# Weight pairs of the last three products: load into two kinds of rooms, with urgent works and a mended joint in the plan

## The chip, the cores and the metric

The kernel runs on one core of a Trainium2 chip. The metric is the device time of one execution in microseconds, the median of the runs; lower is better.

## The reference

Three parts follow each other, all in fp32.

```python
attn = softmax(mask(q @ k.T / 8)) @ v          # 4 x 8 heads x 576 x 64; heads 0-3 see 32 keys back, 4-7 every fourth of 128
x = attn as [2304, 512]
h = x @ w_in                                    # first feed-forward, 512 -> 1024
solu = h * softmax(h); ln = layernorm(solu) * g_ln
x = ln @ w_out                                  # 1024 -> 512
h = x @ w_in2                                   # second feed-forward, 512 -> 2048
g = h * sigmoid(1.702 * h)
out = g @ w_out2                                # 2048 -> 512
```

The change lies in the second feed-forward.

## The kernel before

Products are made of fp32 values split in a high and a low part (hi, lo), so that each product of two blocks is three matmuls for each 128 rows of the sum: hi by hi, hi by lo, lo by hi.

**Tiling.** The 2304 tokens of the second feed-forward are three sets p = 0, 1, 2 of two blocks of 384 tokens. Each set goes through an h stage and then an o stage.

- h stage: eight quads q. A quad multiplies a 2x2 arrangement of blocks by Strassen's scheme with seven products m = 0 to 6 (`h_prod`, L659) of six matmuls, 128x384 each, in four accumulators: two in one two-bank tile hX (tag A of PSUM, tile hx) and two in hZW (tag B, tile hz). Between products the sums are formed by p1 (ACT, L664), u2 (L667), u3 (L671), c22 (L676), c21 (L679) and c12 (L682) on VectorE: m=4 goes into the bank that p1 reads, m=5 needs u3, m=6 needs c22. Then come the sigmoids (`h_sig`, ACT, L688) and the multiplications (`h_mul`, VectorE, L693, L695 and L697 for its parts 0, 1 and 2) that make g. Part 0 is the last to read hX. The inputs of the products are yc (hi by ACT, lo by VectorE, L645) and the weights ws (`quad_load`, L607), four loads a quad.
- o stage of p=0: plain products (`o_plain`, L741), 12 matmuls each, for eight steps jj, two halves and two token blocks b. Block 0 adds up in oa (tag A, both banks of one tile), block 1 in ob (tag B, four tiles). In the same stage the weights of the o stage are read as raw tiles from the input, split in hi and lo (hl tiles) and stored for later.
- o stage of p=1 and p=2: seven products again (`o_prod`, L772), six matmuls for each of the eight jj. The first four, m=0 to 3, run jointly over the eight jj with whole weights wo (`o_load`, L721). The last three, m=4, 5, 6, follow one after the other, each over all eight jj, with weights w that are loaded for a pair of jj at a time (`o_load2`, L758, tiles w2_p_m_jj, two DMAs of 256 KB for a pair): four pairs a product, 144 matmuls in all.
- The operands of the o stage, gs, are the hi part by ACT (L711) and the lo part by VectorE (L714), in five buffers. Sums of g (L707) stand ahead of some of them.

**Order.** A list scheduler (class `Plan`) sets the order of all works. A work has a rank, an engine or several, a cost, the works it comes after, slots it takes and slots it gives back, and a lag until others can use its result. At each time every free engine gets the work of lowest rank that can start. The works are then written out by their planned start, and each engine runs its own in that order. So a work that is not ready holds up all behind it on its engine, whatever the plan had thought.

**Rooms.** Weights lie in rooms of 128x1024. Nine have the slot name hl (`hl_tile`): ws, wo and split weights use them. Three have the name raw: raw weights use them, and in p=1 and p=2 the pairs w. The slots A (2) and B (4) are the banks of PSUM. SyncE issues all DMAs, in order; a load whose room is not free holds up the stores and loads behind it.

In the plain o stage of before the slots A and B are taken by the product of jj = 0 and half 0, and in the o stage of p=1 and p=2 by the product of jj = 0. Another product of the same accumulator was free to stand ahead of it in the plan; `first` in `o_plain` and `o_prod` follows the order that comes out.

Of the kernel before, what the change touches and what calls it, by code (L numbers as in the profile page):

```python
# [9 lines left out]
F32R = mybir.dt.float32r  # L10
# [8 lines left out]
P = 128  # L19
# [30 lines left out]
class Work:  # L50

    def __init__(self, n, rank, can, after, take, give, lag):
        self.key, self.can, self.lag = (rank, n), can, lag
        self.after, self.take, self.give = [w for w in after if w is not None], take, give
        self.start = self.done = None


class Plan:  # L60
# [11 lines left out]
    def order(self):  # L72
# [6 lines left out]
        while any(left.values()):  # L79
# [4 lines left out]
            for eng, works in left.items():  # L84
                while free[eng] <= t:
                    for w in works:
                        if all(a.done is not None and a.done <= t for a in w.after) and \
                                all(slots[s] >= w.take.count(s) for s in w.take) and \
                                (slots["port"] or not w.can[eng][2]) and \
                                all(t + w.can[eng][0] <= max(free[e], t) + c for e, (c, _, _) in w.can.items()):  # L90
                            break
                    else:
                        break
# [33 lines left out]
def attention_moe_kernel(ctx, tc, qk, qk_last, v, v_last, masks, w_in, w_out, g_ln, w2_in, w2_out, out):  # L127
# [623 lines left out]

    def o_load2(p, m, jj):

        t = stage[0].tile([P, 2, 2, 2 * P], F32R, tag="raw", bufs=NRAW, name=f"w2_{p}_{m}_{jj}")
        at_ = (2, 4, 14)[m - 4] * P
        for k in range(2):
            w2t[m, jj + k] = t[:, k]
            nc.sync.dma_start(f32(t[:, k]), wd["o", jj + k].rearrange("p (d c) -> p d c", d=2)[:, :, at_:at_ + 2 * P])  # L758
# [261 lines left out]
    for p in range(3):  # L1020
# [4 lines left out]
        for n, q in enumerate(QUADS):  # L1025
# [18 lines left out]
            for m in range(7):  # L1044
# [26 lines left out]
                for key in held if m == 6 else ():  # L1071
                    hl_end[key] = w
            muls[q] = [s0, s1, s2]
        last_m = [prods[QUADS[-1], m] for m in range(7)]
        y_free = last_m
# [11 lines left out]
        for jj in range(NQ if p == 0 else 0):  # L1087
# [14 lines left out]
            for b in range(2):  # L1102
                for half in range(2):
# [4 lines left out]
                            give=("gs", "hl", "hl") if b and half else ("gs",))  # L1108
                    now[jj, 2 * half + b] = x
            for d in range(2):  # L1110
                hl_end[(("o", jj, d), 0) if ("o", jj, d) in KEEP else (p, "o", jj, d)] = x
                if ("o", jj, d) in KEEP:
                    x.after.append(stored[("o", jj, d), 0])
# [13 lines left out]
        for jj in range(NQ):  # L1127
# [15 lines left out]
            for m in range(4):  # L1143
                x = add(r, "PE", 1.042, lambda p=p, jj=jj, m=m: o_prod(p, jj, m), loads + [ops[m], prods[QUADS[-1], 3]],
                        take=(("A",), ("A",), ("B", "B"), ("B", "B"))[m] if jj == 0 else (),
                        give=("gs", "hl", "hl") if m == 3 else ("gs",))
                now[jj, m] = x
            for d in range(2):
                hl_end[p, "o", jj, d] = x
        end_ = [[now[jj, m] for jj in range(NQ)] for m in range(4)]  # L1150

        def store(c, ws):
            add(r, "SP", 1.3, lambda p=p, c=c: o_store(p, c), ws, give=("sg",), lag=2.0)
# [5 lines left out]
        for d in range(2):  # L1159
            c22.append(add(r, "DVE", 0.53, lambda p=p, d=d: o_out(p, 0, d), end_[3] + [u3[d]] + c22, give=("u3",),  # L1160
                           take=() if d else ("sg",)))
        store(0, c22)
        wait = {4: p1, 5: u3, 6: c22}
        for m in (4, 5, 6):
            xs_ = []
            for jj in range(NQ):
                r = r0 + 10 * (NQ * (m - 3) + jj)
                if jj % 2 == 0:
                    w = add(r - 60, "SP", 1.7, lambda p=p, m=m, jj=jj: o_load2(p, m, jj),
                            [stored[("o", jj + k, d), part] for k in range(2) for d in range(2) for part in range(2)] +  # L1170
                            [now[1, 0]], take=("raw",), lag=2.0)
                if m == 4:
# [5 lines left out]
                else:  # L1178
                    op = operand(jj, m, 1, 1, muls[jj] + [gsum[jj, 0], gsum[jj, 2], gsum[jj, 3]], give=("g",))
                x = add(r, "PE", 1.042, lambda p=p, m=m, jj=jj: o_prod(p, jj, m), [w, op] + wait[m] + end_[3],  # L1180
                        give=("gs", "raw") if jj % 2 else ("gs",))
                xs_.append(x)
# [190 lines left out]
```

## Time and profile before

| | us |
|---|---|
| runs | 684.74 (median), 684.17, 687.91 |
| profiled execution | 682.37 |
| its span | 680.6 |
| TensorE busy in the span | 653.5 (96%) |
| VectorE busy | 522.7 (77%) |
| ACT busy | 387.7 (57%) |

The durations come from the profiled execution, whose span leaves out 1.8 us around it. The second feed-forward begins at about 300 us: p=0 until 438.55, p=1 until 558.05, p=2 to the end. In a timeline a row that says x12 is a run of 12 instructions of one kind that lie close together, and the time in brackets is how long the engine had waited ahead of it and for whom.

### The profile page before, as it was taken

To read this page: it belongs to the slowest core of one execution; us is meant where nothing else is said; L and a number is where in the kernel's file an instruction comes from. 1 tells how busy PE (TensorE), PEld (TensorE's weight loads), DVE (VectorE), ACT (ScalarE), POOL (GpSimd) and SP (SyncE) were. 2 spreads that over 40 slices of the span, in tenths; PEclk is the share of its full clock that TensorE was granted. 3 is DMA by queue.
4 is the path that set the end of the run, shared out by engine and by line. 5 is a ranking of instruction groups with operands and counts; after the bars stand their busy time and mean duration, and the time that the engine had idled before them with its cause. 6 is when DMAs were issued, how large, how long until landed. Compare 5 with 4: busy or idle time off the path is not lost.

```text
span 680.6 us, 12937 instructions
## 1 busy us (share of the span) xinstructions
PE 653.5 (96%) x4921; PEld 616.4 (91%) x4921; DVE 522.7 (77%) x948; ACT 387.7 (57%) x789; POOL 127.6 (19%) x148
## 2 busy tenths in 40 slices
PE   6788999999999999999997999999999999999997
PEld 5666898888888899999997999999999989999996
DVE  3999968775676899789666899387699848668783
ACT  4898877675566786865335676243366424334552
POOL 0305464362433452523000000000000000000000
PEclk9999999999999999999998999999999999999999
DMA  9998226544322667985674877876799865678655
GB/s 292 309 306 259 73 85 213 187 140 149 100 65 89 245 210 266 325 313 196 248 271 160 332 270 249 323 268 227 276 311 317 281 199 213 222 264 321 194 180 192
DMA packets 58254, 155.55 MB, mean 229 GB/s; under 512 B 6608, under 2 KB 21968, under 8 KB 58192
## 3 DMA queue, kind: packets, MB, share of 16 engines
q1 hardware_dynamic: 58192, 154.72, 66.6%
q8 instruction: 39, 0.64, 0.4%
q14 instruction: 23, 0.19, 0.1%
HBM read 118.53 MB, written 36.18 MB: 227 GB/s over the span
## 4 chain that ended last, share of the span: by engine, by line
PE 86%; DMA 6%; DVE 4%; ACT 2%; issue 1%; SPq 0%; POOL 0%; POOLq 0%; ACTq 0%; DVEq 0%
PE h L465 15%; PE hz L659 15%; PE y L538 13%; PE hx L659 11%; PE oz L772 8%; PE ox L772 7%; PE ob L741 5%; PE oa L741 5%; DMA w<-wdo 3%; PE lt L516 2%; PE ptp L309 2%; PE xt L325 2%; PE s L228 1%; DMA y<-in_qk_dram 1%; DMA raw_('o', 1, 1)_3957<-in_w_out_dram 1%
## 5 line engine op out<-in xcount | busy, mean ns | idle before, releaser
L711 ACT CAST gs<-g 128x384 fp32r<-128x384 f32 x144 | 73.2, 513 | 71.8 <-PE oz L772 26.1
L659 PE MATMUL hz<-yc,ws 128*128 128x384 f32 x576 | 109.1, 337 | 0.0
L659 PEld LDWEIGHTS hz<-yc,ws 128*128 128x128 f32 x576 | 102.0, 190 | 0.2 <-DVE g L676 0.2
L714 DVE TENSOR_TENSOR gs<-g,gs 128x384 fp32r<-128x384 f32 x144 | 78.4, 555 | 19.4 <-ACT gs L711 18.8
L659 PE MATMUL hx<-yc,ws 128*128 128x384 f32 x432 | 83.4, 335 | 0.9 <-DVE yc L645 0.5
L538 PE MATMUL y<-lnh,wo_h 128*128 128x256 f32 x288 | 83.0, 288 | 0.0
L538 PE MATMUL y<-lnh,wo_l 128*128 128x256 f32 x288 | 81.5, 283 | 0.0
L538 PE MATMUL y<-lnl,wo_h 128*128 128x256 f32 x288 | 81.5, 283 | 0.0
L659 PEld LDWEIGHTS hx<-yc,ws 128*128 128x128 f32 x432 | 75.4, 188 | 1.8 <-DVE yc L645 0.8
L465 PE MATMUL h<-wi_h,xh 128*128 128x512 f32 x144 | 59.0, 410 | 0.0
L465 PE MATMUL h<-wi_l,xh 128*128 128x512 f32 x144 | 56.4, 392 | 0.0
L465 PE MATMUL h<-wi_h,xl 128*128 128x512 f32 x144 | 56.4, 392 | 0.0
L538 PEld LDWEIGHTS y<-lnh,wo_h 128*128 128x128 f32 x288 | 55.1, 191 | 1.0
L538 PEld LDWEIGHTS y<-lnl,wo_h 128*128 128x128 f32 x288 | 55.2, 192 | 0.3
L538 PEld LDWEIGHTS y<-lnh,wo_l 128*128 128x128 f32 x288 | 55.1, 191 | 0.0
L688 ACT ACTIVATE sg<-g 128x768 f32<-128x768 f32 (+1 forms) x48 | 32.9, 686 | 31.8 <-DVE g L679 27.5
L688 ACT ACTIVATE sg<-hx 128x384 f32<-128x384 f32 x24 | 11.8, 492 | 49.7 <-PE hx L659 46.8
L772 PE MATMUL oz<-gs,w 128*128 128x384 f32 x192 | 34.9, 337 | 2.0 <-DMA w<-wdo 1.3
L772 PE MATMUL oz<-gs,wo 128*128 128x384 f32 x192 | 36.7, 335 | 0.0
L772 PE MATMUL ox<-gs,wo 128*128 128x384 f32 x192 | 36.5, 334 | 0.0
L772 PEld LDWEIGHTS oz<-gs,w 128*128 128x128 f32 x192 | 33.1, 188 | 3.4 <-issue 2.5
L301 POOL TENSOR_TENSOR t<-t,sx 128x768 f32<-128x768 f32 (+1 forms) x17 | 23.7, 1392 | 65.0 <-DVE sx L296 25.1
(391 smaller groups left out, 1408.9 us busy)
## 6 DMA issues: line engine op xcount, KB each, us to landing
ws<-wdq SPq DMA_DIRECT2D x48, 512.0 KB, 4.8
wo<-wdo SPq DMA_DIRECT2D x37, 512.0 KB, 5.5
ws<-wdq SPq DMA_DIRECT2D x48, 384.0 KB, 5.2
w<-wdo SPq DMA_DIRECT2D x48, 256.0 KB, 4.4
qk<-in_qk_dram SPq DMA_DIRECT2D x14, 528.0 KB, 5.5
v<-in_v_dram SPq DMA_DIRECT2D x14, 384.0 KB, 4.1
y<-in_w_in_dram SPq DMA_DIRECT2D x9, 512.0 KB, 5.0
wdq<-y SPq DMA_DIRECT2D x9, 512.0 KB, 3.2
```

The lines of the kernel that those rows point to most:

```text
L301: eng.tensor_tensor(t, t, wide(sms.pop(n), t.shape[1]), ALU.mult)
L309: nc.tensor.transpose(ps[:, j * P:j * P + P], t[:, 4 * h + j, :], ident)
L325: nc.tensor.matmul(ps[64 * h:64 * h + 64, w * QW:w * QW + QW], vW[4 * b + u][:, h, w, :], pt[:, h, w * QW:w * QW + QW], start=True, stop=True)
L465: nc.tensor.matmul(hps[i][:, half, :], x[:, kt, :], w[:, kt, fs], start=(kt == 0 and j == 0), stop=(kt == KT - 1 and j == 2))
L516: nc.tensor.transpose(ps[:, j, :], es[i][:, f * P:f * P + P], ident)
L538: nc.tensor.matmul(yps[g, dm][:, 0:n], w[:, f, ds_], x[:, f, 0:n], start=(f == 0 and j == 0), stop=(f == NF1 - 1 and j == 2))
L659: nc.tensor.matmul(ps[:, 0:TB2], quad_weights(q, m, kk, a), yc2[m][:, x, kk, :], start=(m < 4 and kk == 0 and i == 0), stop=(kk == 1 and i ...
L688: nc.scalar.activation(sg, src, AF.Sigmoid, scale=1.702)
L711: nc.scalar.copy(gsp[jj, m][:, 0], o_block(jj, half, b))
L714: nc.vector.tensor_tensor(gsp[jj, m][:, 1], o_block(jj, half, b), f32(gsp[jj, m][:, 0]), ALU.subtract)
L741: nc.tensor.matmul(ps, w[:, (2 * k + a) * P:(2 * k + a + 1) * P], gsp[jj, 2 * half + b][:, x], start=first and i == 0, stop=last and i == 2)
L772: nc.tensor.matmul(ps, w, gsp[jj, m][:, x], start=m < 4 and first and i == 0, stop=last and i == 2, skip_group_check=True)
```

## The change

Three things are changed.

1. The weight pairs of the last three products go by turns into a room of the kind hl (pairs 0 and 2 of a product) and one of the kind raw (pairs 1 and 3). In the plan a pair costs SyncE 1.4 instead of 1.7 and lands 3.8 instead of 2.0 after it.
2. Some works are called urgent: p1, u2, u3, c22 and the first multiplication of each quad, and p1, u2, u3, c22 of the o stage. When VectorE is free, the plan passes over a work whose rank is 5 or more behind an urgent one, if the urgent one becomes ready while that work would still run for over 0.2 us.
3. The product that takes the accumulator's slots must be the first: all others of the same accumulator come after it.

```diff
--- before.py
+++ after.py
@@ class Work
+        self.urgent = False
@@ class Plan, order
             for eng, works in left.items():
                 while free[eng] <= t:
+                    soon = [(x.key[0], max(a.done for a in x.after)) for x in works if x.urgent and
+                            all(a.done is not None for a in x.after) and
+                            all(slots[s] >= x.take.count(s) for s in x.take)] if eng == "DVE" else []
                     for w in works:
+                        if any(t < r < t + w.can[eng][0] - 0.2 and w.key[0] - k >= 5 for k, r in soon):
+                            continue
                         if all(a.done is not None and a.done <= t for a in w.after) and \
@@ attention_moe_kernel, o_load2
-    def o_load2(p, m, jj):
-
-        t = stage[0].tile([P, 2, 2, 2 * P], F32R, tag="raw", bufs=NRAW, name=f"w2_{p}_{m}_{jj}")
+    def o_load2(m, jj, t):
+
+        t = t.rearrange("p (k d c) -> p k d c", k=2, d=2)
         at_ = (2, 4, 14)[m - 4] * P
@@ h quads, behind the seven products
             muls[q] = [s0, s1, s2]
+            for w in (p1, u2, u3, c22, s0):
+                w.urgent = True
@@ plain o stage (p=0)
                     now[jj, 2 * half + b] = x
+                    if jj or half:
+                        x.after.append(now[0, b])
@@ o stage of p=1, 2: first four products
                 now[jj, m] = x
+                if jj:
+                    x.after.append(now[0, m])
@@ o stage of p=1, 2: outputs
+        for w in p1 + u2 + u3 + c22:
+            w.urgent = True
         store(0, c22)
@@ o stage of p=1, 2: last three products
                 if jj % 2 == 0:
-                    w = add(r - 60, "SP", 1.7, lambda p=p, m=m, jj=jj: o_load2(p, m, jj),
+                    room = ("hl", "raw")[jj // 2 % 2]
+
+                    def load(p=p, m=m, jj=jj, room=room):
+                        o_load2(m, jj, hl_tile(f"w2_{p}_{m}_{jj}", hi_now[p, m, jj], hl_end[p, m, jj]) if room == "hl" else
+                                stage[0].tile([P, 1024], F32R, tag="raw", bufs=NRAW, name=f"w2_{p}_{m}_{jj}"))
+                    hi_now[p, m, jj] = w = add(r - 60, "SP", 1.4, load,
                             [stored[("o", jj + k, d), part] for k in range(2) for d in range(2) for part in range(2)] +
-                            [now[1, 0]], take=("raw",), lag=2.0)
+                            [now[1, 0]], take=(room,), lag=3.8)
@@
                 x = add(r, "PE", 1.042, lambda p=p, m=m, jj=jj: o_prod(p, jj, m), [w, op] + wait[m] + end_[3],
-                        give=("gs", "raw") if jj % 2 else ("gs",))
+                        give=("gs", room) if jj % 2 else ("gs",))
+                hl_end[p, m, jj - jj % 2] = x
                 xs_.append(x)
```

The number of instructions stays. TensorE's order changes from m=4 of quad 7 of p=0 into the start of the plain o stage, in quad 0 of p=1 and in the o stage of p=1; in p=2 it is the same. Line numbers of after are 7 higher.

**TensorE, the joint of p=0.** Names: hx0_7, hz0_7 are the accumulators of quad 7, oa and ob those of the o stage, gs2_jj_k the operand of step jj, where k is 2 half + b. From the end of m=4, before:

```order
L659 MATMUL hx0_7_4554<-yc0_4_3849,ws0_7_0_0_4462 128x384 x3
L659 MATMUL hx0_7_4554<-yc0_4_3849,ws0_7_1_0_4503 128x384 x3
L741 MATMUL oa0_4615<-gs2_0_2_4143,wo0_0_0_4550 128x384 x3
L741 MATMUL oa0_4615<-gs2_0_2_4143,hl_('o', 0, 1)_0_4562 128x384 x3
L741 MATMUL oa1_4616<-gs2_0_2_4143,wo0_0_0_4550 128x384 x3
L741 MATMUL oa1_4616<-gs2_0_2_4143,hl_('o', 0, 1)_0_4562 128x384 x3
L659 MATMUL hz0_7_2_4578<-yc0_5_4026,ws0_7_0_0_4462 128x384 x3
L659 MATMUL hz0_7_2_4578<-yc0_5_4026,ws0_7_1_0_4503 128x384 x3
L659 MATMUL hz0_7_3_4592<-yc0_6_3841,ws0_7_0_1_4489 128x384 x3
L659 MATMUL hz0_7_3_4592<-yc0_6_3841,ws0_7_1_1_4514 128x384 x3
L741 MATMUL ob00_4665<-gs2_0_3_4156,wo0_0_0_4550 128x384 x3
L741 MATMUL ob01_4666<-gs2_0_3_4156,hl_('o', 0, 1)_0_4562 128x384 x3
```

and after:

```order
L666 MATMUL hx0_7_4554<-yc0_4_3849,ws0_7_0_0_4462 128x384 x3
L666 MATMUL hx0_7_4554<-yc0_4_3849,ws0_7_1_0_4503 128x384 x3
L666 MATMUL hz0_7_2_4578<-yc0_5_4026,ws0_7_0_0_4462 128x384 x3
L666 MATMUL hz0_7_2_4578<-yc0_5_4026,ws0_7_1_0_4503 128x384 x3
L666 MATMUL hz0_7_3_4592<-yc0_6_3841,ws0_7_0_1_4489 128x384 x3
L666 MATMUL hz0_7_3_4592<-yc0_6_3841,ws0_7_1_1_4514 128x384 x3
L748 MATMUL oa0_4644<-gs2_0_0_4137,wo0_0_0_4550 128x384 x3
L748 MATMUL oa0_4644<-gs2_0_0_4137,hl_('o', 0, 1)_0_4562 128x384 x3
L748 MATMUL oa1_4645<-gs2_0_0_4137,wo0_0_0_4550 128x384 x3
L748 MATMUL oa1_4645<-gs2_0_0_4137,hl_('o', 0, 1)_0_4562 128x384 x3
L748 MATMUL oa0_4644<-gs2_0_2_4149,wo0_0_0_4550 128x384 x3
L748 MATMUL oa0_4644<-gs2_0_2_4149,hl_('o', 0, 1)_0_4562 128x384 x3
```

Products 5 and 6 of quad 7 (hz0_7) have moved ahead of the first o product, and the o stage starts with gs2_0_0 instead of gs2_0_2.

**VectorE, the same place**, from u2 (p10_7) of quad 7 on. Before:

```order
L667 TENSOR_TENSOR p10_7_4590<-hx0_7_4554,p10_7_4590 128x384
L645 TENSOR_TENSOR yc1_0_4599<-y1_1_80,yc1_0_4599 128x2x256
L645 TENSOR_TENSOR yc1_0_4599<-y1_2_81,yc1_0_4599 128x2x128
L671 TENSOR_TENSOR u30_7_4633<-hz0_7_2_4578,p10_7_4590 128x384
L634 TENSOR_TENSOR y1_1_80<-y1_2_81,y1_1_80 128x2x256
L676 TENSOR_TENSOR g0_15_4639<-hz0_7_3_4592,u30_7_4633 128x384
L634 TENSOR_TENSOR y1_2_81<-y1_2_81 128x2x128
L645 TENSOR_TENSOR yc1_2_4611<-y1_2_81,yc1_2_4611 128x768
L598 TENSOR_TENSOR hl_('o', 1, 0)_1_4647<-raw_('o', 1, 0)_3883,hl_('o', 1, 0)_1_4647 128x4x128
L693 TENSOR_TENSOR g0_7_4638<-hx0_7_4554,sg0_7_0_4651 128x384
L679 TENSOR_TENSOR g0_15_4639<-hz0_7_2_4578,p10_7_4590 128x384
```

and after:

```order
L674 TENSOR_TENSOR p10_7_4590<-hx0_7_4554,p10_7_4590 128x384
L678 TENSOR_TENSOR u30_7_4613<-hz0_7_2_4578,p10_7_4590 128x384
L683 TENSOR_TENSOR g0_15_4620<-hz0_7_3_4592,u30_7_4613 128x384
L652 TENSOR_TENSOR yc1_0_4599<-y1_1_80,yc1_0_4599 128x2x256
L652 TENSOR_TENSOR yc1_0_4599<-y1_2_81,yc1_0_4599 128x2x128
L700 TENSOR_TENSOR g0_7_4619<-hx0_7_4554,sg0_7_0_4630 128x384
L686 TENSOR_TENSOR g0_15_4620<-hz0_7_2_4578,p10_7_4590 128x384
L641 TENSOR_TENSOR y1_1_80<-y1_2_81,y1_1_80 128x2x256
L605 TENSOR_TENSOR hl_('o', 1, 0)_1_4641<-raw_('o', 1, 0)_3883,hl_('o', 1, 0)_1_4641 128x4x128
```

u3 (u30_7) and c22 (g0_15<-hz0_7_3) follow u2 at once, and h_mul part 0 (g0_7<-hx0_7) has gone ahead of the y sums and the split of hl_('o', 1, 0)_1; yc1_2 has left this place.

**TensorE, quad 0 of p=1.** Each product is two rows. From m=1 on, before:

```order
L659 MATMUL hx1_0_5327<-yc1_1_4662,ws1_0_0_1_5244 128x384 x3
L659 MATMUL hx1_0_5327<-yc1_1_4662,ws1_0_1_1_5275 128x384 x3
L659 MATMUL hz1_0_2_5351<-yc1_2_4611,ws1_0_0_1_5244 128x384 x3
L659 MATMUL hz1_0_2_5351<-yc1_2_4611,ws1_0_1_1_5275 128x384 x3
L659 MATMUL hz1_0_3_5361<-yc1_3_4959,ws1_0_0_1_5244 128x384 x3
L659 MATMUL hz1_0_3_5361<-yc1_3_4959,ws1_0_1_1_5275 128x384 x3
L659 MATMUL hx1_0_5327<-yc1_4_4630,ws1_0_0_0_5202 128x384 x3
L659 MATMUL hx1_0_5327<-yc1_4_4630,ws1_0_1_0_5261 128x384 x3
```

and after:

```order
L666 MATMUL hx1_0_5327<-yc1_1_4805,ws1_0_0_1_5258 128x384 x3
L666 MATMUL hx1_0_5327<-yc1_1_4805,ws1_0_1_1_5275 128x384 x3
L666 MATMUL hx1_0_5327<-yc1_4_4616,ws1_0_0_0_5220 128x384 x3
L666 MATMUL hx1_0_5327<-yc1_4_4616,ws1_0_1_0_5261 128x384 x3
L666 MATMUL hz1_0_2_5358<-yc1_2_4611,ws1_0_0_1_5258 128x384 x3
L666 MATMUL hz1_0_2_5358<-yc1_2_4611,ws1_0_1_1_5275 128x384 x3
L666 MATMUL hz1_0_3_5367<-yc1_3_5003,ws1_0_0_1_5258 128x384 x3
L666 MATMUL hz1_0_3_5367<-yc1_3_5003,ws1_0_1_1_5275 128x384 x3
```

m=4 (yc1_4) has moved from behind m=3 to ahead of m=2 (yc1_2).

**Queue of SyncE, last three products of p=1.** ws2 are the weights of the h stage of p=2, out the stores. Before, nine ws2 loads end here, behind three pairs:

```order
L607 DMA ws2_1_1_0_6310<-wdq1_109 128x768
L607 DMA ws2_1_1_1_6330<-wdq1_109 128x1024
L607 DMA ws2_2_0_0_6345<-wdq2_110 128x768
L799 DMA out_0_dram<-ob1_0_6334 128x2x384
L758 DMA w2_1_4_6_6369<-wdo6_122 128x2x256
L758 DMA w2_1_4_6_6369<-wdo7_123 128x2x256
L758 DMA w2_1_5_0_6391<-wdo0_116 128x2x256
L758 DMA w2_1_5_0_6391<-wdo1_117 128x2x256
L758 DMA w2_1_5_2_6400<-wdo2_118 128x2x256
L758 DMA w2_1_5_2_6400<-wdo3_119 128x2x256
```

and after:

```order
L765 DMA w2_1_5_4_6248<-wdo4_120 128x2x256
L765 DMA w2_1_5_4_6248<-wdo5_121 128x2x256
L765 DMA w2_1_6_0_6261<-wdo0_116 128x2x256
L765 DMA w2_1_6_0_6261<-wdo1_117 128x2x256
L765 DMA w2_1_6_4_6285<-wdo4_120 128x2x256
L765 DMA w2_1_6_4_6285<-wdo5_121 128x2x256
L614 DMA ws2_0_0_0_6298<-wdq0_108 128x768
L614 DMA ws2_0_0_1_6336<-wdq0_108 128x1024
L614 DMA ws2_0_1_0_6351<-wdq0_108 128x768
L806 DMA out_0_dram<-ob1_0_6340 128x2x384
L614 DMA ws2_0_1_1_6375<-wdq0_108 128x1024
L765 DMA w2_1_5_6_6388<-wdo6_122 128x2x256
L765 DMA w2_1_5_6_6388<-wdo7_123 128x2x256
```

Nine pairs (w2_1_4_2 to w2_1_6_4) stand ahead of the first ws2 load and the first store; pair 6 of m=5 and, further down, pairs 2 and 6 of m=6 come between ws2 loads. Before, the first store stood ahead of nine pairs.

## Rows read from the trace of the kernel before

**Rows 1.** Waits of TensorE, 255 to 681 us: total us, times, longest us.

```profile
PE oa L741 <- DVE g L693: 4.4, 1, 4.4
PE oz L772 <- DMA w<-wdo: 1.3, 3, 0.5
...
PE ox L772 <- DMA w<-wdo: 0.6, 1, 0.6
...
PE hx L659 <- DVE p L667: 0.3, 1, 0.3
```

**Rows 2.** Stretches: us, busy us PE, PEld, DVE, ACT, POOL, granted clock, DMA share, GB/s.

```profile
439.00:497.00 58.00, 58.00 (x337) 58.00 (x336) 42.61 (x79) 22.22 (x40) 0.00 (x0) 1.00 0.75 259
497.00:530.00 33.00, 33.00 (x191) 32.70 (x190) 32.17 (x64) 20.39 (x41) 0.00 (x0) 1.00 0.93 306
530.00:558.00 28.00, 26.42 (x147) 25.06 (x146) 18.15 (x37) 10.65 (x21) 0.00 (x0) 1.00 0.79 259
```

**Rows 3.** Timeline, TensorE, joint of p=0: start us, us, instruction, [idle before <-releaser].

```profile
363.65 0.68 PE L741 MATMUL oa<-gs,wo 128*128 128x384 f32 x3
...
369.27 0.79 PE L741 MATMUL oa<-gs,wo 128*128 128x384 f32 x3 [4.42 <-DVE g L693]
...
370.62 3.60 PE L659 MATMUL hz<-yc,ws 128*128 128x384 f32 x12
374.07 0.68 PE L741 MATMUL ob<-gs,wo 128*128 128x384 f32 x3
```

**Rows 4.** Timeline, VectorE, the same joint.

```profile
363.92 0.56 DVE L667 TENSOR_TENSOR p<-hx,p 128x384 f32<-128x384 f32 x1 [1.54 <-PE hx L659]
364.39 1.02 DVE L645 TENSOR_TENSOR yc<-y,yc 128x512 fp32r<-128x512 f32 x2
...
368.66 0.56 DVE L693 TENSOR_TENSOR g<-hx,sg 128x384 f32<-128x384 f32 x1
```

**Rows 5.** Stretches of 2 us behind the joint: columns as in rows 2.

```profile
370.00:372.00 2.00, 2.00 (x9) 2.00 (x8) 0.00 (x0) 1.14 (x3) 0.00 (x0) 0.54 0.00 0
372.00:374.00 2.00, 2.00 (x9) 2.00 (x8) 1.02 (x2) 1.42 (x4) 0.47 (x1) 0.60 0.00 0
```

**Rows 6.** Timeline, TensorE and ACT, start of p=1.

```profile
438.55 2.24 PE L659 MATMUL hx<-yc,ws 128*128 128x384 f32 x12
440.63 2.24 PE L659 MATMUL hz<-yc,ws 128*128 128x384 f32 x12
...
440.82 0.48 ACT L664 COPY p<-hx 128x384 f32<-128x384 f32 x1 [2.03 <-PE hx L659]
```

**Rows 7.** Timeline, TensorE, last three products of p=1.

```profile
530.33 6.40 PE L772 MATMUL ox<-gs,w 128*128 128x384 f32 x36
537.29 2.50 PE L772 MATMUL ox<-gs,w 128*128 128x384 f32 x12 [0.56 <-DMA w<-wdo]
...
545.59 1.28 PE L772 MATMUL oz<-gs,w 128*128 128x384 f32 x6 [0.60 <-ACT gs L711]
547.25 10.97 PE L772 MATMUL oz<-gs,w 128*128 128x384 f32 x60 [0.37 <-DMA w<-wdo]
558.05 2.24 PE L659 MATMUL hx<-yc,ws 128*128 128x384 f32 x12
```

**Rows 8.** Timeline, queue of SyncE, same stretch: xN counts the DMAs issued.

```profile
516.04 15.28 SPq L607 DMA_DIRECT2D ws<-wdq  x9
...
533.08 7.91 SPq L758 DMA_DIRECT2D w<-wdo  x8
```

**Rows 9.** Timeline, TensorE, last three products of p=2.

```profile
649.91 8.48 PE L772 MATMUL ox<-gs,w 128*128 128x384 f32 x48
...
665.15 8.56 PE L772 MATMUL oz<-gs,w 128*128 128x384 f32 x48 [0.52 <-DMA w<-wdo]
674.16 2.32 PE L772 MATMUL oz<-gs,w 128*128 128x384 f32 x12 [0.44 <-DMA w<-wdo]
```

**Rows 10.** Tile w, the weight pairs: landing.

```profile
DMA to landing us min/median/max: 3.0/4.4/7.4
```

## The prediction

> **What bounds the kernel now.** I read the waits of TensorE first, over the second feed-forward alone (from 255 us on; the change touches nothing before it), then the busy time by stage, then the timelines of TensorE, VectorE and the queue of SyncE around each place where TensorE lost time. The waits are few [rows 1]: one of 4.4 us in the plain o stage of p=0, three DMA waits of 1.3 us together and one of 0.6 us at the last three products of p=1 and p=2, and 0.3 us at an h quad of p=2. All else in this half of the kernel is TensorE at work. So the time can fall only by what is lost at these places, plus what is lost around them, and it can rise at any stage where another engine is nearly full. That one is the o stage of p=1, where VectorE is busy 32.17 of 33 us [rows 2].
>
> My measure of a loss: a matmul of this width starts 0.1733 us after the one before it, since 12 of them lead from 438.55 to 440.63 [rows 6]. What a stretch takes beyond its count times 0.1733 is lost, whether or not it is called a wait.
>
> **Place A, the joint of p=0, quad 7 to the o stage.** Before, TensorE runs m=4 of quad 7, then the first half (oa0) of the o product with operand gs2_0_2, and stands still for 4.42 us before the second half (oa1), until h_mul part 0 (g, L693) is done [rows 3]. This part reads hX of quad 7, whose room in tag A the accumulator is to get. The plan took that room with the product of half 0 only, while the one of half 1 ran first, so the plan did not know of the wait. VectorE meanwhile was never idle: u2 at 363.92, then u3 and c22 with yc, y and hl pieces between and behind them, and h_mul last, 368.66 to 369.22 [rows 4]. From 363.65 to the first ob product at 374.07 pass 10.42 us for 24 matmuls, which are 4.16: 6.26 us are lost. 4.42 of them is the wait, 1.84 the rest: the products behind it ran at a granted clock of 0.54 and 0.60 of full speed [rows 5], that is for the most part at the lower of the two levels, 1.2 GHz, and 12 of them took 3.45 us instead of 2.08 [rows 3].
>
> After, by the order of the instructions, m=5 and m=6 of quad 7 go ahead of every o product, and VectorE does u2, u3 and c22 in a row. I replay this with the durations of [rows 4], 0.56 for u3 and c22 as for u2. u2 starts as before at 363.92 and ends at 364.48; u3, which reads its result, 364.58 to 365.14 (0.1 for the handing over); m=5 can start at 365.2, which is 1.55 after m=4 ended at 363.65. c22 ends at 365.8, before m=5 does (366.24), so m=6 runs without a wait to 367.28. The two yc pieces take VectorE to 366.6 (1.02, [rows 4]), h_mul to 367.2: in time for oa1. **Gain: 6.26 - 1.55 = 4.71**. Bounds: 6.26 if the stall went wholly, 2.87 if the slow clock came back behind the 1.55 (4.71 - 1.84).
>
> The clock decides between these two. The rows: after 4.42 us of rest it fell; over the last three products of p=1, with gaps of 0.37 to 0.60 us, the mean granted clock stayed at 1.00 [rows 2, 7]. The gap of 1.55 lies between, nearer to 0.60, and full work stands on both sides; I take no fall. The Trainium skill (TensorE: Matmul & The Clock Gate, "HAM oscillation — how this bites in real kernels") says that a stream of matmuls broken by idle stretches loses the full clock and has to earn it back at half rate. [...]
>
> In the plain o stage behind it (64 us, no loss before) the operands and weights are prepared further ahead of their use than before, as the loads begin earlier by as much as the joint shortens. I charge nothing. The cover is the five operand buffers.
>
> **Place B, quad 0 of p=1.** The new order puts m=4 ahead of m=2 and m=3. m=4 adds into the bank that ACT has to copy first (p, L664), and that copy waits for m=1: it ran 440.82 to 441.30, m=1 having ended at about 440.63 [rows 6]. Before, m=2 and m=3 covered it. Now TensorE waits: **loss 0.7** (441.30 + 0.05 - 440.63). Bounds 0 and 0.9.
>
> **Urgent works elsewhere.** VectorE no longer starts a long piece when u2, u3 or c22 is about to become ready. At one quad of p=2 this removes the 0.3 us on p, L667 [rows 1]: **gain 0.3**. At quads 0 and 1 of p=0 my replay has pieces that come 0.2 to 0.3 earlier and others that much later: 0, within 0.2 either way. The other quads had no loss, and VectorE has the time for the pieces put off: in the quads of p=1 it is busy 42.61 of 58 us [rows 2].
>
> In the o stage of p=1 VectorE's order changes as well. It has 33 - 32.17 = 0.8 us to spare [rows 2]. Replayed against the products in their new order, the operands come 0.45 to 0.8 us before their use at many products, about at the same time at the last ones, 0.1 late at one. I take **0**, bounds -0.3 and +4 (each us that VectorE idles there beyond 0.8 us is a us of the span).
>
> **Place D, the last three products of p=1.** 144 matmuls from 530.33 to 558.05 take 27.72 instead of 24.96: **2.76 lost**. By the starts [rows 7] they are 0.72 before 537.29, 1.02 before 545.59, 0.62 before 547.25 and 0.40 before the end. The cause is in the queue of SyncE [rows 8]: with three rooms for pairs only three pairs can be loaded ahead; then nine ws loads for p=2 (516.04, 15.28 us) and the first store stand in the queue, and only at 533.08 do the next pairs go out, 4.2 us ahead of their use at 537.29. A pair takes 3.0 to 7.4 us to land, 4.4 in the middle [rows 10]. (The one wait that the trace puts down to ACT's cast, at 545.59, I read as a weight pair too: five operands are made ahead.) After, nine pairs are queued ahead of the first store. Only three stand behind, and each waits for a room that a product gives back long before its use: pair 6 of m=5 after 24 matmuls (4.2 us into the stretch, used at 14.6), pair 2 of m=6 at 8.3 (used at 18.7), pair 6 of m=6 at 12.5 (used at 22.9). So 10.4 us are there for a landing of up to 7.4 and for what stands ahead in the queue. **Gain 2.76**, bounds 0 and 2.76. What goes to the back instead: the ws loads of p=2, all needed at 25 us into the stretch or later; 24 is where the eighth of them goes out, and that belongs to quad 1, first used some 8 us behind it. The load on the DMA engines ahead of 530 doesn't rise: six pairs (6 x 512 KB) come in, nine ws loads (3968 KB) go out.
>
> **Place E, the last three of p=2.** The same, with no ws loads: 84 matmuls from 649.91 should lead to 664.47 and lead to 665.15, and 48 more to 673.47 and lead to 674.16 [rows 9]: 0.68 + 0.69 = **1.37, gained** for the same reason; bounds 0 and 1.37. The stores at the end stay.
>
> **The sum.** -4.71 + 0.7 - 0.3 + 0 - 2.76 - 1.37 = -8.44. The profiled execution took 682.37 with a span of 680.6 (1.8 around it); it becomes 673.9. The median of the runs, 684.74, lies 2.37 above it; I carry that over: **676.3**. By the bounds of A to E alone, everything at its best (6.26 + 0.3 + 0.3 + 2.76 + 1.37 = 11.0) gives 673.7.
>
> **Rivals.**
> - *The clock falls at A behind the 1.55 gap.* For it: rows 5. Against: the gaps of up to 0.60 without a fall. 676.3 + 1.8 = **678.1**. [...]
> - *VectorE bounds the o stage of p=1.* It has 0.8 us to spare in 33; in-order work put behind an urgent piece that is not ready yet idles it, and nothing later in the stage makes up for it. 1 to 4 us: **677 to 680.5**.
> - *The same, so large that the kernel gets slower.* Place: the eight k-steps of four products (4.16 us each) of that stage. Price: one for one beyond 0.8 us of idle VectorE. Point: at 8.4 + 0.8 = 9.2 us of idle time, 1.15 per k-step, all gains are gone; at 1.6 per k-step it is **688**. Against: the pieces are 0.5 us long, and a k-step would have to lose two or three in waiting.
> - *The pairs still come late.* The rooms of the first four products free up only at the end of the stage, all pairs go out close together, and transfers at a share of 0.93 [rows 2] stretch each other beyond 10 us. Then only A, B and the quad are gained, 4.3: **680.4**. Against: no pair took over 7.4 us before.
>
> **How the numbers follow.** 0.58 for the forecast (674.5 to 678), 0.12 for the clock, 0.13 for VectorE at 1 to 4 us, 0.11 for late pairs, 0.06 for slower. 0.5% (3.4 us, about what a measurement of this kernel can tell from no change) divides at 681.3 and 688.2. Below 681.3 lie the first three and some of the fourth, about 0.85 with something off for a median that is loose by 2 us; slower by over 0.5% is 0.05, the rest 0.10. The range from 673.7, where all bounds are at their best, to 680.5 leaves out the slower case, half of the late pairs and a little below, under 2 in 10.
>
> **What would show it.** In the profile after: no wait of oa on g (L700), in its place one of about 1.5 us of hz on u3 (L678) near 365, at clock 1.00 in the 4 us behind; a wait of about 0.7 of hx on ACT's copy (L671) at about 436; the last three products of p=1 in 25.0 us with no DMA wait of w, those of p=2 likewise; the o stage of p=1 at 33.3 us or less. It is wrong if w waits of 0.3 or more remain, if the o stage of p=1 takes over 34.5, if the clock after 365 shows under 0.9, or if a wait on ws or on gs appears where there was none.

## The result, and the profile after

The changed kernel takes 677.01 us in the median of four runs (676.17 to 683.21), the kernel before 684.80 (684.17 to 687.91). The ratio is 0.9892, 95% interval 0.9859 to 0.9925: 7.8 us less, or 5.1 to 9.7 by the interval. The forecast was 676.3, with a range of 673.7 to 680.5. Three runs of the experiments below lie far above the others of their kernel (720.56, 726.48 and 1294.07 us); they count in the medians and not in the ratios.

The profiled execution took 677.7 us, its span is 675.9. Between the two profiled executions lie only 4.7 us, since 2.1 us were lost ahead of everything that the change touches. So I compare stage by stage. Each figure is the time from the first TensorE instruction of a stretch to the first of the next one, in the timelines of the two kernels.

| stretch | before | after | forecast | measured |
|---|---|---|---|---|
| ahead of the first h product | 294.25 | 296.32 | 0 | +2.07 |
| p=0, h quads up to m=4 of quad 7 | 69.40 | 70.00 | 0 | +0.60 |
| the 24 products at the joint (place A) | 10.42 | 5.75 | -4.71 | -4.67 |
| rest of the plain o stage | 64.48 | 65.36 | 0 | +0.88 |
| p=1, h quads (place B) | 58.24 | 59.09 | +0.7 | +0.85 |
| p=1, first four o products | 33.54 | 33.38 | 0 | -0.16 |
| p=1, last three (place D) | 27.72 | 25.27 | -2.76 | -2.45 |
| p=2, h quads and first four | 91.86 | 91.52 | -0.3 | -0.34 |
| p=2, last three (place E) | 26.41 | 24.96 | -1.37 | -1.45 |
| behind the last product | 4.27 | 4.27 | 0 | 0.00 |

From the end of m=4 of quad 7 on the profile gives -7.34, against -8.44 forecast. The first row does not answer to the change, and of the second only a part does, 0.31 us in quad 1 (see urgent works below). The first row varies with the execution: in the eleven profiles of the experiments below it lies between 295.2 and 299.2, and TensorE's mean granted clock in the first 60 us between 0.86 and 0.97; it was 1.00 in the profile of before and 0.91 in that of after. The second holds a wait of 0.8 us on p in quad 0. It varies as well: with and without part 2 the kernels below take 68.5 to 72.5 us there, and the changed kernel itself 72.2 in a second profile.

The waits of TensorE after (total us, times, longest us), answering to [rows 1]:

```profile
PE hz L666 <- DVE u L678: 1.3, 1, 1.3
PE hx L666 <- DVE p L674: 0.8, 1, 0.8
PE ob L748 <- DVE gs L721: 0.6, 1, 0.6
PE hx L666 <- ACT p L671: 0.6, 1, 0.6
```

The 4.4 us on g and all the DMA waits of w are gone; u, gs and ACT's p are new. At the joint, TensorE's timeline (start, us, instruction, idle before and releaser), answering to [rows 3]:

```profile
365.28 1.21 PE L666 MATMUL hx<-yc,ws 128*128 128x384 f32 x6
367.80 2.35 PE L666 MATMUL hz<-yc,ws 128*128 128x384 f32 x12 [1.31 <-DVE u L678]
369.99 0.68 PE L748 MATMUL oa<-gs,wo 128*128 128x384 f32 x3
```

VectorE at the same place, to [rows 4]:

```profile
366.59 0.56 DVE L674 TENSOR_TENSOR p<-hx,p 128x384 f32<-128x384 f32 x1 [1.54 <-PE hx L666]
367.18 0.56 DVE L678 TENSOR_TENSOR u<-hz,p 128x384 f32<-128x384 f32 x1
367.77 0.56 DVE L683 TENSOR_TENSOR g<-hz,u 128x384 f32<-128x384 f32 x1
...
369.18 0.55 DVE L700 TENSOR_TENSOR g<-hx,sg 128x384 f32<-128x384 f32 x1
```

and the stretches of 2 us behind the wait (columns as in [rows 2], the granted clock third from the end), to [rows 5]:

```profile
368.00:370.00 2.00, 2.00 (x13) 2.00 (x13) 2.00 (x5) 0.71 (x2) 0.00 (x0) 1.00 0.88 293
370.00:372.00 2.00, 2.00 (x13) 2.00 (x13) 2.00 (x3) 1.63 (x3) 1.57 (x1) 1.00 0.77 221
```

u2, u3 and c22 follow each other by 0.59 us, h_mul ends ahead of oa1, and the clock stays at full speed. The first row of VectorE has one thing that I had read past, and it stands in [rows 4] too: u2 waits 1.54 us for hx and starts only when m=4 ends. We come back to it.

The last three products, TensorE, p=1 and then p=2, to [rows 7, 9]:

```profile
529.90 8.79 PE L779 MATMUL ox<-gs,w 128*128 128x384 f32 x48
538.53 16.80 PE L779 MATMUL oz<-gs,w 128*128 128x384 f32 x96
555.17 1.03 PE L666 MATMUL hx<-yc,ws 128*128 128x384 f32 x5
...
646.69 8.48 PE L779 MATMUL ox<-gs,w 128*128 128x384 f32 x48
655.01 16.80 PE L779 MATMUL oz<-gs,w 128*128 128x384 f32 x96
```

and the queue of SyncE in p=1, to [rows 8]:

```profile
513.35 13.65 SPq L765 DMA_DIRECT2D w<-wdo  x16
527.04 3.85 SPq L614 DMA_DIRECT2D ws<-wdq  x3
...
534.56 1.19 SPq L765 DMA_DIRECT2D w<-wdo  x2
...
538.72 1.18 SPq L765 DMA_DIRECT2D w<-wdo  x2
...
542.88 1.19 SPq L765 DMA_DIRECT2D w<-wdo  x2
```

Nine pairs are out by 527 (eight in the first row, one at 510.03); the three others go out at 534.56, 538.72 and 542.88, each 10.2 us ahead of its use (544.77, 548.93 and 553.09, counting products of 1.04 us from 538.53). Landing takes 3.0 to 6.0 us. In p=2 the 144 products run without a gap.

### The profile page after: what moved, and what is told of

The parts are those of the page before. It is cut to its first block, busy times and chain, and to the rows that moved or that the text cites. A ratio compares the mean times of both kernels' runs of the same rounds, so it can differ in the third digit from the quotient of the medians.

```text
span 675.9 us, 12935 instructions
## 1 busy us (share of the span) xinstructions
PE 653.8 (97%) x4921; PEld 617.3 (91%) x4921; DVE 524.2 (78%) x950; ACT 386.6 (57%) x789; POOL 126.3 (19%) x146
## 4 chain that ended last, share of the span: by engine, by line
PE 74%; DVE 11%; DMA 8%; issue 2%; ACT 2%; POOL 1%; SPq 0%; ACTq 0%; DVEq 0%; POOLq 0%
PE hz L666 14%; PE h L472 12%; PE hx L666 11%; PE oz L779 10%; PE y L545 9%; PE ox L779 7%; PE ob L748 2%; PE ptp L316 2%; PE oa L748 2%; PE lt L523 2%; PE xt L332 1%; PE s L235 1%; DMA y<-in_w_in_dram 1%; DMA raw_('o', 3, 0)_4712<-in_w_out_dram 1%; DMA raw_('o', 1, 1)_3957<-in_w_out_dram 1%
## 5 line engine op out<-in xcount | busy, mean ns | idle before, releaser
L666 PE MATMUL hz<-yc,ws 128*128 128x384 f32 x576 | 107.5, 334 | 1.3 <-DVE u L678 1.3
L666 PEld LDWEIGHTS hz<-yc,ws 128*128 128x128 f32 x576 | 100.5, 188 | 1.6 <-DVE u L678 1.6
L779 PEld LDWEIGHTS oz<-gs,wo 128*128 128x128 f32 x192 | 33.5, 188 | 0.2 <-DVE gs L721 0.2
```

The lines of the kernel that those rows point to most:

```text
L666: nc.tensor.matmul(ps[:, 0:TB2], quad_weights(q, m, kk, a), yc2[m][:, x, kk, :], start=(m < 4 and kk == 0 and i == 0), stop=(kk == 1 and i ...
L779: nc.tensor.matmul(ps, w, gsp[jj, m][:, x], start=m < 4 and first and i == 0, stop=last and i == 2, skip_group_check=True)
```

## Experiments

The parts one at a time, on the kernel before; then each left out of the changed kernel; then the two costs that showed. Times are medians of the runs, ratios are to the kernel before on the same chip.

**Part 1 alone.**

```diff
-                    w = add(r - 60, "SP", 1.7, lambda p=p, m=m, jj=jj: o_load2(p, m, jj),
+                    room = ("hl", "raw")[jj // 2 % 2]
...
+                    hi_now[p, m, jj] = w = add(r - 60, "SP", 1.4, load,
...
-                            [now[1, 0]], take=("raw",), lag=2.0)
+                            [now[1, 0]], take=(room,), lag=3.8)
```

> The kernel before with part 1 alone (rooms by turns, cost 1.4, lag 3.8 for the weight pairs). Theory (the parts act at separate places and add up): the last three products of p=1 fall from 27.72 to 25.0-25.3 us and those of p=2 from 26.33 to 25.0; the joint of p=0 stays as before, with a wait of about 4.4 us of oa on g and slowed products behind it; sum -4.0 us, about 680.8. Rival (the pairs come early only because the other parts move the o stage): the DMA waits of w stay, within 1 us of before.

681.24 us, ratio 0.9945 (0.9927 to 0.9963). TensorE's waits from 300 us on, and the last three products of p=1:

```profile
PE oa L741 <- DVE g L693: 4.4, 1, 4.4
```

```profile
533.28 8.48 PE L772 MATMUL ox<-gs,w 128*128 128x384 f32 x48
541.60 16.80 PE L772 MATMUL oz<-gs,w 128*128 128x384 f32 x96
558.24 2.07 PE L659 MATMUL hx<-yc,ws 128*128 128x384 f32 x11
```

One wait is left, the one at the joint, and the last three products take 24.96 us in p=1 and 24.95 in p=2. The rooms alone bring D and E, wholly. The wait that the trace of before had put down to ACT's cast [rows 7] went with them: it was a weight pair.

**Part 2 alone.**

```diff
+                    soon = [(x.key[0], max(a.done for a in x.after)) for x in works if x.urgent and
...
+                        if any(t < r < t + w.can[eng][0] - 0.2 and w.key[0] - k >= 5 for k, r in soon):
+                            continue
...
+            for w in (p1, u2, u3, c22, s0):
+                w.urgent = True
...
+        for w in p1 + u2 + u3 + c22:
+            w.urgent = True
```

> The kernel before with part 2 alone (urgent works). TensorE's order at the joint of p=0 stays that of before, but u2, u3, c22 come in a row on VectorE. Theory: h_mul part 0 ends near 3.3 us after m=4's end instead of 5.6, the wait of oa on g falls from 4.4 to about 2.5 us; if the products behind it run at full clock, 3.7 us are gained there, if they run slow 1.9. The DMA waits at the last three products stay. About 681 to 683.

683.76 us, 0.9974 (0.9952 to 0.9996), a little above the 681 to 683 expected. The rest at the joint is 2.26 us, the 24 products take 6.72, and the clock stayed at full speed behind it (stretches of 2 us):

```profile
370.00:372.00 2.00, 1.16 (x6) 1.16 (x7) 1.98 (x4) 0.00 (x0) 0.00 (x0) 1.00 0.49 184
372.00:374.00 2.00, 2.00 (x13) 2.00 (x13) 0.75 (x2) 0.75 (x2) 0.00 (x0) 1.00 0.62 236
```

3.70 us are gained there; 1.27 go again in the rest of the plain o stage (65.75 against 64.48). The last three products stay at 27.29 and 26.63.

**Part 3 alone.**

```diff
+                    if jj or half:
+                        x.after.append(now[0, b])
...
+                if jj:
+                    x.after.append(now[0, m])
```

> The kernel before with part 3 alone (the product that takes the slots comes first). TensorE's order at the joint has m=5, m=6 ahead of oa; VectorE has yc between u2 and u3 as before. Theory: m=5 waits about 2.3 us for u3, oa1 another 0.3 for h_mul; 6.26 lost there becomes 2.6, so -3.6 us (-1.8 if the clock falls behind the wait); DMA waits at the last three products stay; no m=4 ahead of m=2 in quad 0 of p=1, so no loss there. About 681.

683.44 us, 0.9973 (0.9954 to 0.9991). TensorE at the joint:

```profile
365.17 1.20 PE L659 MATMUL hx<-yc,ws 128*128 128x384 f32 x6
368.49 3.39 PE L659 MATMUL hz<-yc,ws 128*128 128x384 f32 x12 [2.12 <-DVE u L671]
371.68 1.16 PE L741 MATMUL oa<-gs,wo 128*128 128x384 f32 x3
```

The rest is 2.12 us, and this time the 12 products behind it run slowly (3.19 us from 368.49 to 371.68, for 2.08): 8.16 for the 24, a gain of 2.26, nearer to the lower of my two cases. The last three products take 27.29 and 26.00.

**Without part 1.** The changed kernel with the pairs all in rooms raw again.

> The changed kernel without part 1 (pairs all in rooms raw, cost and lag of before). Theory: the joint of p=0 as in the changed kernel (one wait of 1.3 us), 0.6 us lost in quad 0 of p=1, and the last three products as before: 27.7 and 26.3 us with DMA waits of w. 3.8 us above the changed kernel, about 681. Rival (the rooms only help because of the other parts, or the reverse): within 1 us of the changed kernel.

682.36 us, 0.9939 (0.9911 to 0.9967). The last three products take 27.89 and 26.27 us. Waits:

```profile
PE oz L778 <- DMA w<-wdo: 1.7, 2, 1.3
PE hz L665 <- DVE u L677: 1.3, 1, 1.3
PE ob L747 <- DVE gs L720: 1.1, 1, 1.1
PE hx L665 <- ACT p L670: 0.6, 1, 0.6
PE ox L778 <- DMA w<-wdo: 0.2, 1, 0.2
```

From the joint on, the list is that of the changed kernel with the waits of w added: the places are separate, as the theory has it. The rooms are worth 0.0055 alone and 0.0047 with the rest, 3.2 to 3.8 us.

**Without part 2.** The changed kernel with no work urgent.

> The changed kernel without part 2 (no urgent works). Theory: joint of p=0 loses 2.6 us instead of 1.55 (yc stands between u2 and u3 again), but quad 0 of p=1 keeps m=2 ahead of m=4 and loses nothing (changed kernel 0.6 to 0.85), and the start of the last three products of p=1 loses nothing (0.3). So the urgent works bring nothing on the whole: within 1 us of the changed kernel, about 677. Rival (urgent works carry the gain at the joint): 2 us or more above it.

677.10 us, 0.9885 (0.9862 to 0.9908): the runs do not tell it from the changed kernel. Rest at the joint 2.12 us, 8.12 for the 24 products (at the low clock for a part), 2.37 more than in the changed kernel; the quads of p=1 take 58.58 instead of 59.09, the last three of p=1 24.96 instead of 25.27. By these stages of one profile 2 us should be missing; the runs do not show them. The profiled execution, 680.07 us, is the slowest of the six. Whether the clock falls less often in the other runs I did not settle.

**Without part 3.** The changed kernel with the old order at the joint.

> The changed kernel without part 3 (the old order of the joint, urgent works on VectorE, pairs in both kinds of rooms). Theory: wait of oa on g about 2.5 us at the joint, the last three products without DMA waits. 1 us above the changed kernel if the clock holds behind 2.5 us, 2.8 if not: 678 to 680.

680.01 us, 0.9908 (0.9879 to 0.9937). This interval overlaps that of the changed kernel, so the runs alone do not show that part 3 adds to the other two; the profile does, at the joint. The joint has the order and the rest of part 2 alone, 2.26 us, and here the clock fell:

```profile
372.00:374.00 2.00, 1.51 (x7) 1.51 (x8) 1.63 (x3) 0.07 (x1) 0.00 (x0) 0.89 0.31 121
374.00:376.00 2.00, 2.00 (x8) 2.00 (x8) 0.15 (x1) 0.44 (x1) 0.00 (x0) 0.50 0.75 266
```

8.27 us for the 24 products, where part 2 alone had 6.72 and the changed kernel 5.75. The profiled execution, 682.06 us, is again the slowest of the six.

**What a longer rest costs.** u3 of quad 7 of p=0 is computed six times.

```diff
+        for _ in range(5 if (p, q) == (0, QUADS[-1]) else 0):
+            nc.vector.tensor_tensor(hU3[q], hZW[q, 2][:, 0:TB2], hp1[q], ALU.add)
         nc.vector.tensor_tensor(hU3[q], hZW[q, 2][:, 0:TB2], hp1[q], ALU.add)
```

> The changed kernel with u3 of quad 7 of p=0 computed six times instead of once, so that TensorE rests about 4.3 us at the joint instead of 1.3. Theory (a rest of over 4 us brings the low clock, which costs 1.8 us in the products behind it): the rest grows by 3.0, and the time by 4.5 to 5, with a granted clock near 0.5 to 0.6 in the 4 us behind it. Rival (the 1.84 us of before had another cause than the rest): the time grows by 3.0 and the clock stays at 1.00.

682.89 us, 0.9971 (0.9952 to 0.9990): by the ratios some 5.4 us above the changed kernel, more than the 4.5 to 5 expected. The rest is 4.27 us, and behind it:

```profile
372.00:374.00 2.00, 0.16 (x1) 0.16 (x1) 1.86 (x5) 0.00 (x0) 0.00 (x0) 0.65 0.49 186
374.00:376.00 2.00, 2.00 (x7) 2.00 (x8) 1.78 (x4) 0.00 (x0) 0.00 (x0) 0.50 0.00 0
```

The 24 products take 11.29 us, 5.54 more than in the changed kernel: 2.96 of rest, 2.58 of slower products. Only u3 was repeated, so the slow products belong to the rest that it makes; by the same sign I put the 1.84 us of before down to its rest.

**m=4 after u2.** u2 and m=4 touch two banks of one tile, hX. m=4 writes the bank that p1 copies; u2 reads the other one, which m=1 had written. In the kernels so far the one that is written out second waits for the other, and in quad 7 of p=0 m=4 was first.

```diff
                 if m >= 4:
-                    after.append((p1, u3, c22)[m - 4])
+                    after.append((u2, u3, c22)[m - 4])
```

> The changed kernel, and in the plan m=4 of an h quad comes after u2 instead of p1. Reason: u2 and m=4 use the same tile hX (different banks), so whichever is written out first makes the other wait; in quad 7 of p=0 u2 waited for m=4 though m=1 had long been done. Theory: u2 of quad 7 starts 1.5 us earlier, the wait of 1.3 us at the joint of p=0 falls to 0.4 or less, and m=4 of quad 0 of p=1 goes back behind m=3, which removes 0.6: -1.5 us, about 675.5. Rival (u2 waits for VectorE's own earlier pieces or for ACT): no gain at the joint.

674.97 us, 0.9849 (0.9828 to 0.9871). VectorE and TensorE at the joint:

```profile
363.09 0.55 DVE L674 TENSOR_TENSOR p<-hx,p 128x384 f32<-128x384 f32 x1
363.75 0.56 DVE L678 TENSOR_TENSOR u<-hz,p 128x384 f32<-128x384 f32 x1
```

```profile
363.70 1.32 PE L666 MATMUL hx<-yc,ws 128*128 128x384 f32 x6
364.86 2.24 PE L666 MATMUL hz<-yc,ws 128*128 128x384 f32 x12
366.94 0.68 PE L748 MATMUL oa<-gs,wo 128*128 128x384 f32 x3
```

u2 starts ahead of m=4 and no longer waits for it; m=5 follows m=4 at once, and from the start of m=5 the 24 products take 4.16 us. What is left stands ahead of m=4, which now waits for u2: 0.40 us are lost at its start, too short for the trace to name a wait. In quad 0 of p=1 m=4 is back behind m=3 (58.24). From 300 us on the trace names no wait of TensorE at all. This version is below both kernels, though its interval just overlaps that of the changed kernel. By the stages it is 2.9 us shorter than the changed kernel from m=4 of quad 7 on: 1.2 at the joint, 0.85 in quad 0 of p=1, and 0.88 in the rest of the plain o stage, which lost nothing here though no edit aimed at it.

**The rest of the plain o stage.** The changed kernel again, and the changed kernel with a longer landing time in the plan for the raw weights of this stage.

```diff
-            w = add(r, "SP", W_T, fetch, w_after, take=(raw,), lag=2.0)
+            w = add(r, "SP", W_T, fetch, w_after, take=(raw,),
+                    lag=4.0 if k == 3 and u in (('o', 3, 0), ('o', 3, 1), ('o', 4, 0), ('o', 5, 0), ('o', 5, 1), ('o', 6, 1), ('o', 7, 1)) else 2.0)
```

> The changed kernel once more, beside the next two. Theory (the stages behind the joint repeat to 0.1 us, the part ahead of the second feed-forward does not): rest of 1.3 us at the joint at full clock, 0.3 lost at the start of the last three products of p=1, 59.1 us for the quads of p=1; between 0.4 and 1.4 us lost in the plain o stage; about 677.

678.08 us, 0.9884 (0.9856 to 0.9912). All stages behind the joint repeat to 0.02 us but one: the rest of the plain o stage takes 66.13, 1.65 more than before. In the first profile of the changed kernel one sees how, in ACT, VectorE and TensorE:

```profile
405.60 0.67 ACT L377 ACTIVATE raw_('o', 6, 1)_4986<-raw_('o', 6, 1)_4986 128x512 f32<-128x512 f32 x1 [0.99 <-DMA raw_('o', 6, 1)_4986<-in_w_out_dram]
```

```profile
406.83 0.69 DVE L605 TENSOR_TENSOR hl_('o', 5, 0)_1_5045<-raw_('o', 5, 0)_4915,hl_('o', 5, 0)_1_5045 128x512 fp32r<-128x512 f32 x1 [1.03 <-ACT hl_('o', 5, 0)_1_5045 L601]
...
409.85 0.55 DVE L721 TENSOR_TENSOR gs<-g,gs 128x384 fp32r<-128x384 f32 x1
```

```profile
410.45 0.61 PE L748 MATMUL ob<-gs,hl_('o', 4, 0)_0_4942 128*128 128x384 f32 x2 [0.61 <-DVE gs L721]
```

ACT stands 0.99 us for raw weights that have not landed; behind it VectorE stands 1.03 for ACT; the operand gs comes 0.61 late.

> The changed kernel, with the raw weight loads of the plain o stage planned to land 4.0 instead of 2.0 us after their issue (they take 5.3 to 7.0). Theory (the 0.9 us lost in the plain o stage come from raw loads that ACT waits for while operand casts stand behind them): the plain o stage falls from 65.4 to 64.5-64.8 us; all else as in the changed kernel; -0.6 to -0.9 us. Rival (VectorE's total work in the stage is the cause): no change in the stage.

677.39 us, 0.9888 (0.9861 to 0.9914). The rest of the plain o stage falls to 64.48, with no loss, as the theory has it (one profile; the edit also changes the order of ACT and VectorE in the stage). But the time stays, since the longest wait is now

```profile
PE hx L666 <- DMA ws<-wdq: 2.4, 1, 2.4
```

In SyncE's queue the ws loads for the first quads of p=1 have come behind the stores of the outputs. Two go out at 427.38, the next two only behind two stores, and TensorE stands in quad 0 until one of these lands, 6.5 us after it went out:

```profile
430.84 1.43 SPq L806 DMA_DIRECT2D out_dram<-op  x2
432.32 1.32 SPq L614 DMA_DIRECT2D ws<-wdq  x2
```

```profile
438.86 0.79 PE L666 MATMUL hx<-yc,ws 128*128 128x384 f32 x3 [2.39 <-DMA ws<-wdq]
```

In the changed kernel six stood ahead of the stores:

```profile
426.15 4.12 SPq L614 DMA_DIRECT2D ws<-wdq  x6
433.52 1.43 SPq L806 DMA_DIRECT2D out_dram<-op  x2
```

So the quads of p=1 take 60.93 us. What one stage gained the next gave back.

> Both edits: m=4 of an h quad after u2, and the longer landing time for the raw loads of the plain o stage. Theory: from m=4 of quad 7 on only some 0.4 us are lost (start of the last three products of p=1), as with the first edit alone, so within 0.5 us of it: about 675, 0.985 of the kernel before. Rival: the new order of ACT's work delays operands elsewhere and loses over 0.5.

675.65 us, 0.9863 (0.9836 to 0.9889); the runs do not tell it from the first edit alone. It loses nothing in the plain o stage (64.48), and 1.2 us in the first two quads of p=1 (59.47), where ws comes late again. So the rival's loss of over 0.5 came, by way of SyncE's queue and not of ACT's.

## Why the prediction was right, point by point

**Bounds.** Right for the gains, which came at the places named, with a small one of 0.16 us in the o stage of p=1 besides. Not right for what can rise: 0.88 us were lost anew in the plain o stage, where VectorE was busy 49.50 of 64 us before, and 0.31 each at two smaller places named below.

**Place A.** Right in order, cause and size: 5.75 us for the 24 products, where the replay has 4.16 + 1.55. The clock stayed at 1.00 behind the new rest in all four profiles with a rest of 1.31 us. Part 2 and part 3 work on the same rest: 4.42 before, 2.26 with the one, 2.12 with the other, 1.31 with both. So at the joint they overlap: by the profiles 3.70 us alone and 2.26 alone, 4.67 together. The runs are too loose to show this: the three parts alone bring 0.0055, 0.0026 and 0.0027, which is the whole 0.0108, while on top of the other two only part 1 is clear of the noise.

**Rest of the plain o stage.** Here the step failed. I charged nothing and named the five operand buffers as the cover. The loss was 0.88 us, 1.65 in a second profile, and with it came a sign that the prediction had named for being wrong, a wait on gs where there was none. Operands can be made ahead only if ACT and VectorE get to them, and these stood in their queues behind raw weights that landed later than the plan has it; in the last run but one, with the loads planned to land later, both the waits of ACT for them and the loss were gone but for 0.33 us of ACT. The waits alone don't make the loss: in the profile of before and in that of m=4 after u2 ACT waits for raw weights too, up to 1.37 and 1.75 us, and TensorE loses nothing. What has to come together with them, an operand close behind in the order, is argued from the rows above and was not tested apart.

**Place B.** Right: 0.85 lost in the quads of p=1 (0.57 of it the wait for ACT's copy), 0.7 forecast; it goes when m=4 comes after u2. The copy starts at 439.71, when m=1 has ended, though it reads the bank of m=0: by the code this too is a wait between two banks of one tile, and no run took it out.

**Urgent works elsewhere.** Right in size for p=2 (-0.34 for -0.3), but by luck: the 0.3 us on p that [rows 1] name do not lie in p=2. They are a wait of m=4 in quad 0 of p=0, in the profile before

```profile
311.32 1.31 PE L659 MATMUL hx<-yc,ws 128*128 128x384 f32 x6 [0.35 <-DVE p L667]
```

and it is 0.83 there in the profile after. What went in p=2 is a loss of 0.31 ahead of m=4 of quad 2, too short to be named. The same 0.31 came anew ahead of m=4 of quad 1 of p=0, where the prediction had 0, within 0.2 either way: all nine profiles with part 2 have it there and not in p=2, the four without have it in p=2 and not there. Right for the o stage of p=1 (-0.16 for 0): VectorE at 97% held, and neither size of that rival came. Missed: the first four outputs u2, u3 and c22 of the o stage are urgent too and hold the operands of the next product back. In the profile after:

```profile
528.95 1.02 DVE L787 TENSOR_TENSOR op<-ox,op 128x384 f32<-128x384 f32 x2
...
531.75 0.55 DVE L721 TENSOR_TENSOR gs<-g,gs 128x384 fp32r<-128x384 f32 x1
```

For 2.8 us no gs is made; TensorE loses 0.31 at the start of the last three products. All nine profiles with part 2 lose 0.29 to 0.43 there, the four without nothing.

**Place D and E.** Right: -2.45 and -1.45, for -2.76 and -1.37; the 0.31 are the piece just named, and at E the last 12 products of before had lost another 0.08. Nearly all of it comes from part 1, which alone brings both stretches to 24.96; without it they stay at 27.89 and 26.27.

**The sum.** -8.44 forecast; -7.8 by the medians, -7.0 by the stages with quad 1 of p=0. The terms that were off are +0.88 in the plain o stage, +0.31 at the start of D, +0.31 in quad 1 of p=0 and +0.15 at B; small ones of -0.2 go the other way. That the median came within 0.7 us is in part luck: the profiled execution, forecast at 673.9, took 677.7, and the 2.37 between profile and median that the forecast carried over belongs to a profile of before with the shortest start of all (294.25). The cause of the rest at A that the replay took for granted, u2 waiting for m=4, was the larger oversight: it was a wait between two banks of one tile that no data asked for. Removing it, which mends place B as well, gave 2.0 us at the two places by the profiles.

**The rival of the clock** didn't come with this kernel, but it is real: the clock fell in three of the four profiles with a rest of 2.1 to 2.3 us.

## What to carry to other kernels

Where two engines touch different banks of one tile, look which is written out first: in this kernel the other waited for it, and a row "idle before" that names an instruction whose data isn't read was the sign. A load that the plan expects too early cost nothing here where it was late itself, but in what stood behind the instruction that waited for it, on that engine and on the next. And a loss removed at one stage is only gained when the queue that feeds the next stage has not been pushed back by it.

## What the runs showed of the hardware

I had not expected the clock to fall after so short a rest, nor to do so in some executions only. Rests of TensorE at the joint, each in one profile (lost beyond it is what the 24 products took over 4.16 us and the rest):

| kernel | rest | lost beyond it | lowest granted clock in a stretch of 1 us behind |
|---|---|---|---|
| after (again; with the longer landing time; without part 1) | 1.31 | 0.28 (0.28; 0.30; 0.30) | 1.00 |
| part 3 alone | 2.12 | 1.88 | 0.50 |
| without part 2 | 2.12 | 1.84 | 0.50 |
| part 2 alone | 2.26 | 0.30 | 1.00 |
| without part 3 | 2.26 | 1.85 | 0.50 |
| u3 six times | 4.27 | 2.86 | 0.50 |
| before | 4.42 | 1.84 | 0.50 |
| part 1 alone | 4.42 | 2.94 | 0.50 |

The same order and the same rest of 2.26 us gave both outcomes. Where the clock fell, to 1.2 GHz, 1.8 to 2.9 us are lost beyond the rest, against 0.3 where it stayed up; the size does not follow the rest, since the same 4.42 us gave 1.84 and 2.94. The Trainium skill (TensorE: Matmul & The Clock Gate, "HAM oscillation — how this bites in real kernels") has idle stretches as the cause. The traces agree for the rests of 4.27 and 4.42 us; it has the clock fall only behind longer stretches than the 2.12 to 2.26 us that were enough here in three of four profiles, and there the measurement decides.
